# Memory attention and gated convolution on one core: convolution and x by halves of the tokens, for both head groups side by side

## The chip, the cores and the metric

The kernel runs on one core of a Trainium2 chip. The metric is device time in microseconds (us), the median of three runs. A profiled execution of the same program gives the rows below; its own time is named beside its span.

## What is computed

Eight batches, each with 8 heads, 576 tokens, head width 64 and 32 memory slots; then a gated convolution over 512 channels.

```
a    = softmax(phi, over the tokens)                  # [b,h,s,m]
k_m, v_m = a^T k, a^T v                               # [b,h,m,d]
attn = softmax(q k_m^T / 8, over the slots)           # [b,h,s,m]
x    = attn v_m, heads side by side                   # [b,s,512]
gate = sigmoid(sum_k conv_w[k] * x[s-4+k])            # 5 taps per channel
out  = (gate * (x w_val)) w_out                       # [b,s,512]
```

## The kernel before

All tensors are 32 bits wide. The 8 heads form two groups g of 4 heads (4 x 32 slots = 128 partitions); the 576 tokens form two halves s of 288; the 512 channels form four tiles t of 128, two per group. A line of text, `ORDER`, lists every step of all batches, and the steps are issued in that order, so each engine's queue is the list filtered to that engine. A star at a step's end picks its other engine (`pick`, L211).

Per batch b: `slots` (L398) sums a^T[k v 1] per group in 20 matmuls; `slots_scale` (L416) divides by the sum and writes k and v twice each; `slots_turn` (L429) transposes them, two transposes per group; `scores` (L444) makes q k_m^T for one group in 8 matmuls; the softmax steps (`scores_turn` to `soft_turn`, L455 to L509) run on VectorE, ScalarE and GpSimd and end in pT, the attention turned so that slots lie on partitions. `val_rows` (L527) makes v_m w_val, so that `value` (L626) yields x w_val from attn directly, in 6 matmuls per (half, tile). `gated` (L637) multiplies by the gate on VectorE, `gated_high` and `gated_low` split the product into two parts, `project` (L656) multiplies by w_out in 12 matmuls, `place` copies out of PSUM and `store` writes to memory.

The convolution of a pair (b, g) has two forms. `conv` (L569) folds the 5 taps into v (`taps`, L559) and lets TensorE do them: 40 matmuls of 32x64x288 into two `cv` tiles in PSUM, then one sigmoid per tile. `mix` (L591) computes x itself in 8 matmuls of 32x64x292, and the taps are applied from PSUM: `tap` 0 on ScalarE (L607), taps 1 to 4 on VectorE (L611), each 128x576, then `open_gate`. The table `MIXED` (L35) takes `mix` for 8 of the 16 pairs. In `conv` the two halves of one head go to different 64-column sides of the array (`(j - s) % HG`, L576); in `mix` they go to the same side (`divmod(j, 2)`, L596). `conv` therefore leaves half the channels of the second half of the tokens swapped; to match, `val_again` (L551) keeps a copy of 64 channels behind each value tile, and `wo_pair` (L337) builds a second copy of w_out with rows swapped, by 12 transfers from SBUF to SBUF on SyncE's queue. There are two `cv` tiles of two PSUM banks each, and both are used by `conv`, `mix`, `scores` and, at the start, `warm` (matmuls with no use but to keep TensorE busy). Four `b` tiles of one bank serve all the rest. Loads and stores are all issued by SyncE (SP). k and v lie in one buffer per group (`kvs`, L178), so a group's next load waits for `slots` of the batch before.

Of the kernel before, what the change touches and what calls it, by code (L numbers as in the profile page):

```python
# [45 lines left out]
narrow_done.v.0 load_q.0.0 phi_sub.0.1* narrow_round.v.3 scores.0.0 scores_turn.0.0 soft_max.0.0 warm.8 soft_sub.0.0*
warm.2 phi_exp.0.1 narrow_size.v.3 load_kv.0.1 slots.0.1 warm.2 soft_exp.0.0 narrow_bits.v.3 narrow_add.v.1
narrow_done.v.1 warm.2 load_w.o.1 narrow_size.o.1 soft_sum.0.0 soft_inv.0.0 place_taps.1 phi_sub.1 spread_taps.0
narrow_add.v.3 phi_exp.1 slots_inv.0.1 slots_scale.0.1 warm.2 slots_turn.0.1 slots_place.0.1 narrow_done.v.3
narrow_bits.o.1 place_taps.0 soft_mul.0.0* load_q.0.1 load_w.o.3 narrow_size.o.3 warm.2 narrow_round.o.3 taps.0.0  # L50
soft_turn.0.0 load_kv.1.0 narrow_round.o.1 narrow_bits.o.3 scores.0.1 scores_turn.0.1 soft_max.0.1 soft_sub.0.1*
soft_high.0.0 val_rows.0 val_high.0.1 val_high.0.0 narrow_add.o.3 val_low.0.1 load_kv.1.1 val_low.0.0 soft_exp.0.1
soft_sum.0.1 soft_inv.0.1* warm.2 conv.0.0 sigmoid.0.1 turn_taps.0 lay_taps.0 sigmoid.0.0 soft_mul.0.1* narrow_add.o.1
soft_turn.0.1 slots.1.0 slots_inv.1.0 slots_scale.1.0* narrow_done.o.1 slots.1.1 soft_low.0.0* load_phi.2 load_w.o.2
soft_high.0.1* taps.0.1 wo_high.1 conv.0.1 val_again.0.0.vwH val_again.0.1.vwH* load_q.1 slots_inv.1.1
# [5 lines left out]
val_rows.1 scores_turn.1.0 wo_high.2 wo_low.2 wo_pair.1.0 val_high.1.0 scores_turn.1.1 value.0.1.1 gated.0.1.1
gated_high.0.1.0 value.0.1.3 val_again.1.0.vwH* wo_pair.0.1 project.0.0.0 soft_max.1 val_high.1.1 soft_sub.1
gated.0.1.3 val_low.1.1 soft_exp.1 phi_sub.2 project.0.0.3 project.0.0.1 val_low.1.0 place.0.0.1 place.0.0.0*
phi_max.3 soft_sum.1 soft_inv.1 project.0.0.2 place.0.0.3 value.0.1.2 soft_mul.1* phi_exp.2 gated.0.1.2
gated_high.0.1.1 soft_turn.1 load_kv.2.0 keep_v.1.1 gated_low.0.1.0 val_again.1.0.vwL slots.2.1 slots_inv.2.1
place.0.0.2 slots.2.0 phi_turn.3 slots_scale.2.1* wo_pair.0.0 val_again.1.1.vwH* mix.1.1 slots_inv.2.0 tap.1.2.0
gated_low.0.1.1 slots_turn.2.1 phi_top.3 phi_spread.3 keep_v.2.1 slots_scale.2.0 soft_high.1* phi_lay.3 tap.1.2.1
tap.1.2.2 slots_place.2.1 tap.1.3.0 tap.1.2.3 slots_turn.2.0 slots_place.2.0 tap.1.2.4 open_gate.1.2 tap.1.3.1
tap.1.3.2 soft_low.1 wo_pair.1.1 project.0.1.1 place.0.1.1 load_q.2 project.0.1.0 load_kv.3.0 place.0.1.0 store.0.1.0
tap.1.3.3 tap.1.3.4 open_gate.1.3 value.1.1.3 project.0.1.2 value.1.1.2 gated.1.1.3 taps.2.0 gated.1.1.2 place.0.1.2*  # L70
gated_high.1.1.1 value.1.0.2 gated.1.0.2 phi_sub.3 conv.1.0 val_again.1.1.vwL value.1.1.1 sigmoid.1.1 gated.1.1.1
sigmoid.1.0 value.1.1.0 gated.1.1.0 load_phi.4 phi_max.4 scores.2.1 phi_exp.3 scores.2.0 scores_turn.2.1 value.1.0.3
scores_turn.2.0 gated.1.0.3 gated_high.1.1.0 gated_low.1.1.0* value.1.0.1 soft_max.2 project.0.1.3 load_kv.3.1
place.0.1.3 value.1.0.0 store.0.1.1 gated_low.1.1.1 gated.1.0.1 gated.1.0.0 gated_high.1.0.0 store.0.0.0 soft_sub.2
slots.3.0 gated_high.1.0.1 gated_low.1.0.0 gated_low.1.0.1 slots_inv.3.0 slots.3.1 phi_turn.4 slots_scale.3.0
soft_exp.2 slots_inv.3.1 phi_top.4 slots_scale.3.1 soft_sum.2 soft_inv.2 load_kv.4.0 soft_mul.2* val_rows.2
project.1.1.3 place.1.1.3 val_high.2.1 project.1.0.3 val_high.2.0 place.1.0.3 keep_v.3.1 store.0.0.1 soft_turn.2
project.1.0.1 val_again.2.0.vwH load_q.3 val_low.2.0 val_again.2.1.vwH* val_low.2.1 load_phi.5 project.1.1.2
place.1.1.2* place.1.0.1* mix.2.1 slots_turn.3.1 tap.2.3.0 slots_place.3.1 tap.2.3.1 store.1.1.1 tap.2.2.0
slots_turn.3.0 slots_place.3.0 val_again.2.1.vwL* load_kv.4.1 val_again.2.0.vwL phi_spread.4 phi_lay.4 soft_high.2  # L80
project.1.1.1 place.1.1.1 tap.2.2.1 phi_sub.4 phi_exp.4 project.1.0.0 project.1.1.0 place.1.1.0 tap.2.3.2 tap.2.3.3
project.1.0.2 tap.2.3.4 open_gate.2.3 val_rows.3 place.1.0.2 val_high.3.1 store.1.0.1 tap.2.2.2 tap.2.2.3 tap.2.2.4
open_gate.2.2 phi_max.5 soft_low.2 place.1.0.0 val_high.3.0 val_again.3.1.vwH conv.2.0 val_low.3.1 taps.3.0*
val_again.3.0.vwH value.2.0.0 sigmoid.2.0 val_low.3.0 gated.2.0.0 sigmoid.2.1 value.2.0.1 gated.2.0.1 scores.3.0
scores.3.1 scores_turn.3.0 scores_turn.3.1 soft_max.3 val_again.3.1.vwL* gated_high.2.0.0 slots.4.1 slots_inv.4.1
slots_scale.4.1* slots.4.0 slots_inv.4.0 value.2.0.2 slots_scale.4.0* gated.2.0.2 value.2.1.2 gated.2.1.2 value.2.0.3
load_phi.6 store.1.0.0 gated.2.0.3 gated_high.2.0.1* gated_low.2.0.0 gated_low.2.0.1* value.2.1.1 gated.2.1.1
soft_sub.3 soft_exp.3 soft_sum.3 soft_inv.3 value.2.1.3 project.2.0.1 place.2.0.1 soft_mul.3* gated.2.1.3 soft_turn.3
value.2.1.0 project.2.0.0 place.2.0.0 project.2.0.3 gated.2.1.0 gated_high.2.1.0 phi_turn.5 mix.3.1 phi_top.5
place.2.0.3* tap.3.2.0 gated_low.2.1.0* tap.3.3.0 gated_high.2.1.1* gated_low.2.1.1 phi_spread.5 tap.3.2.1 tap.3.2.2  # L90
tap.3.2.3 tap.3.3.1 load_kv.5.1 tap.3.3.2 tap.3.3.3 store.1.1.0 phi_lay.5 slots_turn.4.1 keep_v.4.1 load_kv.5.0
slots_turn.4.0 project.2.0.2 tap.3.2.4 project.2.1.3 place.2.0.2 val_again.3.0.vwL* soft_high.3 phi_sub.5
slots_place.4.0 project.2.1.2 place.2.1.2 load_q.4 project.2.1.0 tap.3.3.4 scores.4.0 slots_place.4.1 scores.4.1
phi_exp.5 scores_turn.4.0 scores_turn.4.1 soft_max.4 val_rows.4 store.2.0.0 place.2.1.3 store.2.1.1 val_high.4.1*
place.2.1.0 project.2.1.1 val_high.4.0 taps.4.0* place.2.1.1 open_gate.3.2 soft_low.3 value.3.0.2 val_again.4.0.vwH
# [626 lines left out]
```

## Time and profile before

| | |
|---|---|
| time, median of 3 runs | 268.93 us (268.8 to 272.24) |
| time of the profiled execution | 271.08 us |
| its span, first to last instruction | 269.3 us |
| TensorE (PE) busy | 250.1 us, 93% |
| VectorE (DVE) busy | 206.9 us, 77% |
| ScalarE (ACT) busy | 140.5 us, 52% |
| GpSimd (POOL) busy | 116.2 us, 43% |
[...]

Busy time counts any moment with at least one instruction in flight; matmuls overlap, so TensorE's price of a step is read from the chain of waits, where steps follow each other without overlap. A 32-bit matmul shows as two records: 8 matmuls of `mix` are "x16". "Start to start" is the distance of the starts of successive instructions.

### The profile page before, as it was taken

Reading aid. Unit: us, or ns where it says so; the run is one execution under the profiler, and the core shown is the slowest. Engines: PE = TensorE matmul, PEld = TensorE weight load, DVE = VectorE, ACT = ScalarE, POOL = GpSimd, SP = SyncE. Lnnn points to the kernel's source line nnn. Section 1 sums busy time; section 2 is a strip of 40 time slices with the busy share of each in tenths; the row PEclk is TensorE's granted clock in tenths of the full one; section 3 lists DMA queues with packets and bytes.
Section 4 is the critical chain, followed back from the end, with each engine's and each line's share of the span. In section 5 each row is a group of like instructions: output and inputs, shape, how many; then the busy total and the mean of one; then the engine's idle time right before and its main releaser. Section 6 shows DMA issues by size and latency. Waiting matters only on the chain.

```text
span 269.3 us, 7274 instructions
## 1 busy us (share of the span) xinstructions
PE 250.1 (93%) x3096; PEld 216.0 (80%) x3096; DVE 206.9 (77%) x338; ACT 140.5 (52%) x245; POOL 116.2 (43%) x94
## 2 busy tenths in 40 slices
PE   0599959995999999999999999999999999999995
PEld 0387757793988887798789996999879878899994
DVE  2678978996759979789886777789577987898831
ACT  3726764762745558445685346636458565364210
POOL 4466613892921616323635540743237144461200
PEclk9999989998999999999999999999999999999999
DMA  6999987698681992099407268088143210102123
GB/s 203 407 357 355 320 339 247 156 240 234 249 318 60 333 352 99 15 325 347 167 12 217 103 223 267 0 287 334 44 142 127 77 56 2 44 2 88 46 88 131
DMA packets 13232, 49.91 MB, mean 185 GB/s; under 512 B 1673, under 2 KB 2185, under 8 KB 10257
## 3 DMA queue, kind: packets, MB, share of 16 engines
q1 hardware_dynamic: 13200, 49.46, 53.7%
q8 instruction: 24, 0.39, 0.6%
q14 instruction: 8, 0.06, 0.1%
HBM read 37.92 MB, written 9.44 MB: 176 GB/s over the span
## 4 chain that ended last, share of the span: by engine, by line
PE 83%; DMA 10%; issue 2%; ACT 2%; SPq 1%; DVE 1%; DVEq 0%; ACTq 0%
PE b L661 36%; PE b L632 18%; PE cv L577 8%; DMA kv<-in_kv_dram 8%; PE b L403 7%; PE cv L597 4%; PE cv L449 3%; PE b L532 2%; DMA e<-in_phi_dram 2%; PE b L433 2%; PE cv L226 1%; PE b L360 1%; SPq L259 1%; ACT hH L216 1%; DVE h L640 0%
## 5 line engine op out<-in xcount | busy, mean ns | idle before, releaser
L661 PE MATMUL b<-hL,woH 128*128 128x288 f32 x256 | 76.6, 299 | 0.0
L661 PE MATMUL b<-hH,woL 128*128 128x288 f32 x256 | 75.5, 295 | 0.0
L661 PE MATMUL b<-hH,woH 128*128 128x288 f32 x256 | 75.4, 294 | 0.0
L219 POOL TENSOR_TENSOR hL<-h,hH 128x576 fp32r<-128x576 f32 x22 | 32.6, 1488 | 60.0 <-ACT hH L216 32.2
L611 DVE SCALAR_TENSOR_TENSOR gate<-cv,cwP,gate 128x576 f32<-128x576 f32 x64 | 50.0, 813 | 5.9 <-ACT gate L607 4.8
L661 PEld LDWEIGHTS b<-hL,woH 128*128 128x128 f32 x256 | 48.0, 187 | 2.8 <-issue 1.0
L661 PEld LDWEIGHTS b<-hH,woH 128*128 128x128 f32 x256 | 48.2, 188 | 0.0
L661 PEld LDWEIGHTS b<-hH,woL 128*128 128x128 f32 x256 | 48.1, 188 | 0.0
L216 ACT COPY o<-b 128x288 f32<-128x288 f32 x48 | 18.7, 399 | 49.4 <-PE b L661 32.8
L640 DVE TENSOR_TENSOR h<-b,gate 128x288 f32<-128x288 f32 x64 | 27.9, 452 | 19.1 <-PE b L632 15.8
L632 PE MATMUL b<-pL,vwH 128*128 128x288 f32 x128 | 29.0, 308 | 0.0
L632 PE MATMUL b<-pH,vwH 128*128 128x288 f32 x128 | 27.3, 294 | 0.0
L632 PE MATMUL b<-pH,vwL 128*128 128x288 f32 x128 | 27.3, 294 | 0.0
L403 PE MATMUL b<-kv,e 128*32 128x129 f32 x640 | 21.8, 287 | 5.8 <-DMA kv<-in_kv_dram 3.1
L403 PEld LDWEIGHTS b<-kv,e 128*32 128x32 f32 x640 | 18.6, 139 | 8.9 <-issue 4.8
L632 PEld LDWEIGHTS b<-pL,vwH 128*128 128x128 f32 x128 | 20.1, 188 | 6.2 <-issue 2.4
L219 POOL TENSOR_TENSOR pL<-pT,pH 128x1152 fp32r<-128x1152 f32 x7 | 18.7, 2673 | 14.1 <-DVE pH L216 9.8
L577 PE MATMUL cv<-pT,taps 32*64 32x288 f32 x640 | 22.0, 410 | 0.1
L479 POOL TENSOR_TENSOR st<-st,mm 128x1152 f32<-128x1152 f32 x7 | 14.9, 2134 | 15.9 <-DVE mm L472 15.0
L216 ACT CAST hH<-h 128x576 fp32r<-128x576 f32 x21 | 13.9, 673 | 14.0 <-DVE h L640 14.0
L389 POOL TENSOR_TENSOR e<-e,mxa 128x1280 f32<-128x1280 f32 x7 | 17.2, 2464 | 8.7 <-ACT mxa L216 8.7
L632 PEld LDWEIGHTS b<-pH,vwL 128*128 128x128 f32 x128 | 20.5, 188 | 0.0
(87 smaller groups left out, 414.1 us busy)
## 6 DMA issues: line engine op xcount, KB each, us to landing
kv<-in_kv_dram SPq DMA_DIRECT2D x16, 1032.0 KB, 7.6
out_dram<-o SPq DMA_DIRECT2D x30, 288.0 KB, 2.4
q<-in_q_dram SPq DMA_DIRECT2D x7, 1152.0 KB, 8.4
e<-in_phi_dram SPq DMA_DIRECT2D x7, 640.0 KB, 6.4
kv<-in_kv_dram SPq DMA_DIRECT2D x16, 129.0 KB, 8.3
raw<-in_w_out_dram SPq DMA_DIRECT2D x4, 512.0 KB, 8.0
...
```

Of the source, the lines that this page charges most:

```text
L216: eng.copy(out=out, in_=x) if eng is nc.scalar else eng.tensor_copy(out=out, in_=x)
L219: eng.tensor_tensor(out=out, in0=x, in1=hi.bitcast(F32), op=ALU.subtract)
L389: eng.tensor_tensor(out=t, in0=t, in1=mxa.unsqueeze(3).to_broadcast(list(t.shape)), op=ALU.subtract)
L403: nc.tensor.matmul(km[j * M:(j + 1) * M, 0:2 * D + 1], lhsT=e[:, g, j * M:(j + 1) * M, c], rhs=x[:, c, j, :], start=(c == 0), stop=(c == C ...
L449: nc.tensor.matmul(sc[j * M:(j + 1) * M, s, 0:HALF], lhsT=live["kvT", b, g][rows, 0, j * M:(j + 1) * M], rhs=live["q", b][rows, g, j, :], ...
L479: eng.tensor_tensor(out=st, in0=st, in1=spread(live["mm", b, g], st), op=ALU.subtract)
L577: nc.tensor.matmul(cv[t][x * D:(x + 1) * D, s, 0:HALF], lhsT=w[rows, i, :], rhs=p[rows, g, s * HALF + i:(s + 1) * HALF + i], start=(i == 0 ...
L597: nc.tensor.matmul(cv[t][x * D:(x + 1) * D, s, 0:PAD + HALF], lhsT=live["taps", b, g][rows, 0, :], rhs=pTs[b % 2][rows, g, s * HALF:(s + 1 ...
L611: nc.vector.scalar_tensor_tensor(out=gt, in0=x, scalar=w, in1=gt, op0=ALU.mult, op1=ALU.add)
L632: nc.tensor.matmul(vp[:, 0:HALF], lhsT=a[:, t // PG, n:n + P], rhs=p[:, g, s * HALF:(s + 1) * HALF], start=(i == 0), stop=(i == len(parts) ...
L640: nc.vector.tensor_tensor(out=h[:, i], in0=live["vp", b, s, t][:, 0:HALF], in1=live["gate", b, t][:, s], op=ALU.mult)
L661: nc.tensor.matmul(ps[:, 0:HALF], lhsT=w[:, t, n * P:(n + 1) * P], rhs=a[:, t % 2], start=(i == 0), stop=(i == len(parts) - 1))
```

## The change

`conv` and `mix` now run per (batch, half of the tokens) with both head groups side by side, and which head goes to which side of the array depends on (head + group). No channels are swapped between halves any more: the host lays the last four heads out in the order 5, 4, 7, 6 in w_val, conv_w and w_out. `val_again`, `keep_v`, `wo_pair` and the second copies of w_out are gone. `mix` is taken for 12 of the 16 (batch, half) pairs (was 8 of 16 (batch, group) pairs): both halves in batches 3 to 7, one half in batches 1 and 2. One `gate` tile now holds the two channel tiles of a group for one half, and as every channel tile has its own tap weights, each tap is two instructions of 128x288 (was one of 128x576).

v is written once per batch for both groups (`kvd[:, G, g]`), so `slots_turn` makes three transposes per batch, and `slots_scale` two instructions per group. k and v loads leave out the last 64 tokens, which come in one transfer per batch for both groups (`load_rest`, 264 KB); the main loads rotate over three buffers. `kvd` has 3 buffers (2), `st` 2 (1). In batch 0 the softmax runs by halves too, so it needs q of both groups at its start. `ORDER` is new throughout; by its stars, VectorE has 5 `place` copies (16), 6 `gated_high` (11), 4 `gated_low` (10), 5 `soft_sub` (2), 4 `soft_mul` (7), 1 `soft_high` (4), 0 `val_high` (2), 3 `slots_scale` (9); the rest of each kind is ScalarE's or GpSimd's. `warm` has 12 matmuls (32).

```diff
-MIXED = {(1, 1), (2, 1), (3, 1), (4, 1), (5, 1), (6, 1), (7, 0), (7, 1)}
+KVS = 3
...
-mix.5.1 tap.5.2.0 tap.5.2.1 store.4.0.0 tap.5.3.0 tap.5.3.1 project.4.0.3 tap.5.3.2 tap.5.3.3 tap.5.3.4 place.4.0.3
+place.4.0.1 project.4.0.3 place.4.0.3 tap.5.1.1.4 project.4.0.2 soft_high.5 tap.5.1.0.3 tap.5.1.0.4 mix.5.0
...
     def load_kv(b, g):
-        t = kvs[g]
-        nc.sync.dma_start(out=t[:, 0:C - 1], in_=kv[b, g, 0:S - KL].rearrange("(p c) n -> p c n", c=C - 1))
-        nc.sync.dma_start(out=t[0:KL, C - 1], in_=kv[b, g, S - KL:])
+        t = kvs[(b * G + g) % KVS]
+        nc.sync.dma_start(out=t, in_=kv[b, g])
+    def load_rest(b):
+        nc.sync.dma_start(out=rests[b % 2], in_=rest[b])
...
-    def wo_pair(i, g):
-        nc.sync.dma_start(out=b[0:D], in_=a[D:P])
-        for t in range(PG):
-            nc.sync.dma_start(out=b[D:P, t], in_=a[0:D, (t + 1) % PG])
...
-    def slots_turn(b, g):
-        for x in range(2):
-            nc.tensor.transpose(out=ps[:, x], in_=live["kvd", b, g][:, x], identity=ident)
+    def slots_turn(b):
+        for x in range(G + 1):
+            nc.tensor.transpose(out=ps[:, x], in_=kvd[:, x].rearrange("p y d -> p (y d)"), identity=ident)
...
-    def val_again(b, g, n):
-        high(pick(nc.gpsimd, nc.scalar), live[n, b, g][:, gs, HG * D:], x[:, gs, 0:D])
...
-    def mix(b, g):
-        for s in range(2):
+    def mix(b, s):
+        for g in range(G):
             for j in range(HG):
-                t, x = divmod(j, 2)
-                nc.tensor.matmul(cv[t][x * D:(x + 1) * D, s, 0:PAD + HALF], lhsT=live["taps", b, g][rows, 0, :],
+                rows, x = slice(j * M, (j + 1) * M), (j + g) % 2
+                nc.tensor.matmul(cv[g][x * D:(x + 1) * D, j // 2, 0:PAD + HALF], lhsT=live["kvd", b][rows, G, g],
                                  rhs=pTs[b % 2][rows, g, s * HALF:(s + 1) * HALF + PAD], start=True, stop=True)
...
-    def tap(b, t, i):
-        x, w = live["cv", b, t][:, :, i:i + HALF], cwP[:, i, t:t + 1]
-            nc.vector.scalar_tensor_tensor(out=gt, in0=x, scalar=w, in1=gt, op0=ALU.mult, op1=ALU.add)
+    def tap(b, s, g, i):
+        for t in range(PG):
+            x, w = live["cv", b, s, g][:, t, i:i + HALF], cwP[:, i, g * PG + t:g * PG + t + 1]
+            if i == 0:
+                nc.scalar.activation(out=gt[:, t], in_=x, func=AF.Identity, scale=w)
+            else:
+                nc.vector.scalar_tensor_tensor(out=gt[:, t], in0=x, scalar=w, in1=gt[:, t], op0=ALU.mult, op1=ALU.add)
...
-            n = t % PG * P + (s * D if swapped(b, t // PG) else 0)
+            n = t % PG * P
```

How the instructions stand, at three places. First TensorE in batch 5 before, from the transposes of batch 6 to the first matmuls of a `project` behind `mix.5.1`; `conv.5.0` follows 67 rows later, behind five projections and two values.

```order
L433 MATMUL b<-ident,kvd 128x128 x2
L360 MATMUL b<-ident,mx 128x128 x2
L597 MATMUL cv<-pT_76,taps 64x292 x8
L661 MATMUL b<-hL,woH_88 128x288
L661 MATMUL b<-hH,woL_90 128x288
```

After, from `mix.5.1` to the next projection (L350 and L393 are `phi_turn` and `slots` of later batches); `mix.5.0` (L591 again) follows after 36 rows of L653, that is three projections.

```order
L591 MATMUL cv<-pT_76,kvd 64x292 x8
L350 MATMUL b<-ident,mx 128x128 x2
L393 MATMUL b<-kv_78,e 32x129 x16
L393 MATMUL b<-rest_81,e 32x129 x4
L393 MATMUL b<-kv_79,e 32x129 x16
L393 MATMUL b<-rest_81,e 32x129 x4
L624 MATMUL b<-pL,vwH 128x288 x2
L624 MATMUL b<-pH,vwL 128x288 x2
L624 MATMUL b<-pH,vwH 128x288 x2
L653 MATMUL b<-hL,woH 128x288
```

In place of a `conv` (L577, x40) a second `mix` follows the first, three projections, one value and one batch's `slots` behind it, and it needs the same two `cv` tiles.

Second VectorE at the same place, before: L611 are the taps of `mix.5.1`, L640 the multiplications by the gate.

```order
L219 TENSOR_TENSOR hL<-h,hH 128x576
L611 SCALAR_TENSOR_TENSOR gate<-cv,cwP,gate 128x576 x6
L216 COPY o<-b 128x288
L611 SCALAR_TENSOR_TENSOR gate<-cv,cwP,gate 128x576 x2
L640 TENSOR_TENSOR h<-b,gate 128x288 x2
L216 CAST hH<-h 128x576
L216 COPY o<-b 128x288
```

After: L604 are the taps, L632 the multiplications by the gate; the x6 and the x10 are the 16 instructions of `mix.5.1`, the x8 the first 8 of `mix.5.0`.

```order
L632 TENSOR_TENSOR h<-b,gate 128x288 x3
L357 TENSOR_REDUCE top<-b 128x2
L604 SCALAR_TENSOR_TENSOR gate<-cv,cwP,gate 128x288 x6
L400 TENSOR_SCALAR ri<-b 128x1
L402 RECIPROCAL ri<-ri 128x1
L632 TENSOR_TENSOR h<-b,gate 128x288
L604 SCALAR_TENSOR_TENSOR gate<-cv,cwP,gate 128x288 x10
L400 TENSOR_SCALAR ri<-b 128x1
L402 RECIPROCAL ri<-ri 128x1
L604 SCALAR_TENSOR_TENSOR gate<-cv,cwP,gate 128x288 x8
```

The 8 instructions of 576 columns have become 16 of 288, and a second 16 follow close behind, with fewer copies and casts between them.

Third SyncE's queue, before: k and v of batch 2 (`load_kv.2.1`, L241 and L242 on kv_80, and `load_kv.2.0` on kv_78), with `wo_pair` (L339, L341) around the second.

```order
L236 DMA e<-in_phi_dram 128x1280
L241 DMA kv_80<-in_kv_dram 128x2064
L242 DMA kv_80<-in_kv_dram 64x516
L339 DMA woL_91<-woL_90 64x1024
L341 DMA woL_91<-woL_90 64x512 x2
L339 DMA woH_89<-woH_88 64x1024
L341 DMA woH_89<-woH_88 64x512 x2
L241 DMA kv_78<-in_kv_dram 128x2064
L242 DMA kv_78<-in_kv_dram 64x516
```

After: L235 on kv_79 and kv_80 are k and v of batch 2, L240 the rest of batch 2, L255 the last w_out load.

```order
L235 DMA kv_78<-in_kv_dram 128x2064
L255 DMA raw<-in_w_out_dram 128x1024
L235 DMA kv_79<-in_kv_dram 128x2064
L245 DMA q<-in_q_dram 128x2304
L235 DMA kv_80<-in_kv_dram 128x2064
L230 DMA e<-in_phi_dram 128x1280
L240 DMA rest_81<-in_rest_dram 128x516
```

No transfer from SBUF to SBUF stands ahead of the loads of batch 2, and the first of them goes to a buffer that batch 0 has left.

## Rows read from the trace of the kernel before

**Rows 1.** Page, parts 1 and 2: span; busy us (share) and instructions; granted clock by 40 slices.
```profile
span 269.3 us, 7274 instructions
PE 250.1 (93%) x3096; PEld 216.0 (80%) x3096; DVE 206.9 (77%) x338; ACT 140.5 (52%) x245; POOL 116.2 (43%) x94
PEclk9999989998999999999999999999999999999999
```

**Rows 2.** Chain of waits, start us, us, engine, tile, line: one of each TensorE step.
```profile
76.30 2.61 PE cv L577 x80
...
78.91 1.79 PE b L632 x12
...
80.70 1.13 PE cv L449 x32
...
85.99 2.36 PE b L403 x80
...
96.34 1.15 PE cv L597 x16
...
147.33 6.40 PE b L661 x48
153.73 0.22 PE b L433 x2
```

**Rows 3.** Busy by stretch: us, then PE, PEld, DVE, ACT, POOL busy (instructions), PEclk, DMA share, GB/s.
```profile
0.00:65.87 65.87, 49.78 (x706) 40.21 (x708) 50.02 (x82) 36.81 (x66) 36.02 (x39) 0.97 0.89 284
65.87:242.26 176.39, 176.39 (x2213) 152.56 (x2214) 142.47 (x230) 97.23 (x166) 77.29 (x53) 0.99 0.46 164
242.26:269.30 27.04, 23.90 (x184) 23.18 (x184) 14.38 (x26) 6.48 (x14) 2.86 (x2) 1.00 0.23 88
```

**Rows 4.** SyncE's waits: who waited for whom, us, times, longest.
```profile
SPq L339 <- ACT vwH L216: 7.5, 1, 7.5
```

**Rows 5.** Chain of waits, the two stalls of TensorE.
```profile
35.44 2.72 issue
38.16 2.52 PE b L403 x41
...
52.41 0.60 SPq L341
...
53.05 10.82 DMA kv<-in_kv_dram
...
63.92 1.34 PE b L403 x40
...
65.87 2.15 PE cv L597 x16
```

**Rows 6.** Busy by stretch, as rows 3: behind the second stall, and VectorE's densest 20 us.
```profile
65.00:70.00 5.00, 5.00 (x44) 3.14 (x35) 2.93 (x7) 1.81 (x4) 2.52 (x1) 0.66 0.95 355
120.00:140.00 20.00, 20.00 (x257) 16.72 (x259) 18.12 (x26) 11.81 (x20) 9.37 (x7) 1.00 0.56 198
```

**Rows 7.** Timeline of VectorE, start us, us, line, output<-inputs, count [idle before].
```profile
68.84 6.66 DVE L611 SCALAR_TENSOR_TENSOR gate<-cv,cwP,gate 128x576 f32<-128x576 f32 x8 [1.44 <-ACT gate L607]
...
145.77 0.81 DVE L640 TENSOR_TENSOR h<-b,gate 128x288 f32<-128x288 f32 x2
...
236.30 5.88 DVE L611 SCALAR_TENSOR_TENSOR gate<-cv,cwP,gate 128x576 f32<-128x576 f32 x8
```

**Rows 8.** Groups by form on VectorE and ScalarE: count, busy us, mean ns, idle before.
```profile
L611 DVE SCALAR_TENSOR_TENSOR gate<-cv,cwP,gate 128x576 f32<-128x576 f32 x64 | 50.0, 813 | 5.9 <-ACT gate L607 4.8
L640 DVE TENSOR_TENSOR h<-b,gate 128x288 f32<-128x288 f32 x64 | 27.9, 452 | 19.1 <-PE b L632 15.8 <-ACT gate L616 1.6 <-issue 1.0
L506 DVE TENSOR_TENSOR st<-st,ss 128x1152 f32<-128x1152 f32 x5 | 6.8, 1358 | 0.2
L219 DVE TENSOR_TENSOR hL<-h,hH 128x576 fp32r<-128x576 f32 x10 | 7.6, 767 | 0.1
L506 DVE TENSOR_TENSOR st<-st,ss 128x576 f32<-128x576 f32 x2 | 1.5, 756 | 0.0
L216 DVE COPY o<-b 128x288 f32<-128x288 f32 x16 | 7.0, 451 | 9.5 <-PE b L661 9.5
L216 DVE CAST hH<-h 128x576 fp32r<-128x576 f32 x11 | 5.0, 458 | 0.3
L607 ACT ACTIVATE gate<-cv,cwP 128x576 f32<-128x576 f32 x16 | 11.2, 741 | 10.6 <-PE cv L597 10.5
L216 ACT COPY o<-b 128x288 f32<-128x288 f32 x48 | 18.7, 399 | 49.4 <-PE b L661 32.8 <-issue 15.7 <-ACT mxa L216 0.8
```

More of the change, by code (lines that the diff above doesn't have):

```diff
@@ L46 @@
[L46 to L55, printed above, removed]
@@ L61 @@
[L61 to L70, printed above, removed]
@@ L71 @@
[L71 to L95, printed above, removed]
@@ new lines @@
+slots_place.3 phi_lay.4 project.1.1.0 tap.2.1.0.1 tap.2.1.0.2 tap.2.1.0.3 gated_high.1.0.1 gated_low.1.0.1 place.1.1.0
+store.1.1.0 tap.2.1.0.4 project.1.1.3 tap.2.1.1.0 tap.2.1.1.1 soft_high.2 place.1.1.3 phi_sub.4 soft_low.2
+project.1.0.0 place.1.0.0 tap.2.1.1.2 tap.2.1.1.3 phi_exp.4 val_rows.3 val_high.3.0 val_high.3.1 scores.3.1
+scores_turn.3.1 tap.2.1.1.4 open_gate.2.1.1 load_kv.4.1 store.1.1.1 val_low.3.0 project.1.0.2 scores.3.0 place.1.0.2
+scores_turn.3.0 open_gate.2.1.0 soft_max.3 slots.4.0 slots.4.1 phi_turn.5 soft_sub.3* taps.2.1 soft_exp.3 conv.2.0
@@ new lines @@
+tap.3.1.0.4 value.2.1.2 gated.2.1.0 gated.2.1.3 gated.2.1.2 phi_exp.5 gated_high.2.1.0 gated_low.2.1.0
+gated_high.2.0.1 load_kv.5.1 tap.3.1.1.1 scores.4.1 tap.3.1.1.2 scores_turn.4.1 val_rows.4 place.1.0.1 gated_low.2.0.1
+slots.5.1 gated_high.2.1.1 slots_inv.5.1 val_high.4.0 val_low.4.0 slots_scale.5.1* slots.5.0 tap.3.1.1.3 store.0.1.1
+slots_inv.5.0 slots_scale.5.0* load_rest.6 scores.4.0 scores_turn.4.0 soft_high.3 gated_low.2.1.1 project.2.1.1
+slots_turn.5 tap.3.1.1.4 slots_place.5 place.2.1.1 phi_turn.6 mix.3.0 tap.3.0.0.0 soft_max.4 soft_sub.4 phi_top.6
@@ new lines @@
+open_gate.5.1.0 val_high.6.0 value.5.1.3 gated.5.1.3 value.5.0.0 phi_sub.7 phi_exp.7 val_low.6.0 tap.5.0.1.3
+tap.5.0.1.4 store.4.0.0 project.4.1.2 place.4.1.2 load_q.7 value.5.1.1 soft_sub.6 gated_high.5.1.1 gated.5.0.0
+gated_low.5.1.1 slots.7.1 soft_exp.6 slots_inv.7.1 slots_scale.7.1* soft_sum.6 slots.7.0 slots_inv.7.0
+slots_scale.7.0* project.4.1.3 project.4.1.1 soft_inv.6 soft_mul.6* place.4.1.3 value.5.1.0 soft_turn.6 place.4.1.1
+value.5.0.3 store.4.1.0 mix.6.1 slots_turn.7 gated.5.1.1 gated.5.1.0 gated_high.5.1.0* open_gate.5.0.1 tap.6.1.0.0
```

367 lines of the change are left out of this document (200 added, 167 removed).

## The prediction

> **What bounds the kernel now.** The page first: TensorE is busy 93% of a 269.3 us span, VectorE 77%, and the granted clock is near full all through [rows 1]. Cut at the first `mix` (65.87 us) and the last (242.26 us), the middle of 176.4 us has TensorE in flight for 176.39 us and VectorE for 142.5, that is 81% [rows 3]. The chain of waits says the same: there it is TensorE, step behind step. So in the middle the end is set by the sum of TensorE's steps, and their prices are read from that chain [rows 2]: `conv` 2.61 us (x80), `mix` 1.15 (x16), a `value` 0.80 (1.59 for x12 records), a `project` 1.60 (6.40 for x48), both groups' `scores` 1.13, both groups' `slots` 2.36, a pair of transposes 0.22. Ahead of the middle TensorE stands still twice: 2.72 us at 35.44, then on the load of k and v of batch 2, issued at 53.05 and landed at 63.87, 2.8 us [rows 5]. That load was late because SyncE waited 7.5 us, for ScalarE, with a transfer of `wo_pair` ahead of it [rows 4].
>
> **The change, part by part.** All sums are against the profiled execution's span of 269.3 us.
>
> *TensorE, number of convs.* Eight `conv` and eight `mix` cost 8 x 2.61 + 8 x 1.15 = 30.1 us. Four `conv` and twelve `mix` at today's price would cost 24.2.
>
> *TensorE, price of a mix.* Here the code matters more than the count. A matmul of 32 rows x 64 columns takes one of 4 x 2 places of the array. `conv` uses all 8: its 40 matmuls are 5 rounds of 8, 2.61 us, 0.52 per round. `mix` before sends head j to side j % 2 in both halves, so its 8 matmuls share 4 places and make two rounds: 1.15 us. After, the side is (j + g) % 2, and the 8 matmuls lie on 8 different places: one round. No row shows such a `mix`. Its bounds are 0.52 (a round of `conv`) and 1.15 (no gain); `scores` of one group is 8 matmuls of 288 on 8 places (64 rows x 32 columns), and two of them take 1.13 us [rows 2], so I take 0.57. Twelve at 0.57 and four `conv` make 17.3 us: 12.8 less than before. The bounds of the price leave 13.4 to 5.9.
>
> *TensorE, transposes.* Three per batch in place of four: 8 x 0.11 = 0.9 us less.
>
> *SyncE and the second stall.* `wo_pair` is gone from the queue, and the first load of batch 2 goes to a third buffer. It no longer waits for anything made after batch 0. [...] What is late next in this place is nothing of SyncE's that I see.
>
> *The start.* Batch 0 by halves needs q of both groups before its first softmax, and the loads up to k and v of batch 1 are 11,320 KB against 10,680 KB, counted over the queue. The 10,680 KB had landed at 38.16 us [rows 5], about 0.28 MB per us, so 640 KB are 2.3 us; 0 if other work hides them. I take 1.5 us more. The 20 `warm` matmuls dropped lie in waits for loads; they cost nothing either way.
>
> Without any wait for VectorE the span would be 269.3 - 12.8 - 0.9 - 4.5 + 1.5 = 252.6 us.
>
> *VectorE, the taps.* 64 instructions of 128x576 become 192 of 128x288. A tap that follows a tap of the same `gate` tile starts 0.83 us after it ((6.66 - 0.82) / 7), one that follows a tap of another tile 0.72 us ((5.88 - 0.82) / 7) [rows 7]. Between them lies the wait for the write before. After, the two channel tiles of a tap alternate, so the second distance holds. A product of 1152 columns takes 1.358 us, one of 576 0.756: 0.30 per 288 columns [rows 8]. So half the columns give 0.72 - 0.30 = 0.42. Bounds: 0.36, the distance of two gate multiplications of 288 columns ((0.81 - 0.45) [rows 7]), and 0.54, the 0.83 less 0.30. At 0.42 all taps take 81 us instead of 51.
>
> *VectorE, what is taken off.* 11 copies at 0.451, 5 casts at 0.458 and 6 subtractions at 0.767 go to ScalarE and GpSimd, two products at 1.36 to GpSimd [rows 8]; with the smaller ones, less three `soft_sub` more, some 20 us. ScalarE gains about 19 (11 copies at 0.399, 48 first taps at some 0.40 for 16 at 0.741 [rows 8], casts), to 160 us, 63% of the span: no bound. GpSimd stays near 119.
>
> *VectorE against TensorE.* In the middle, 7 mixes before and 11 after: 56 taps at 0.79 leave (44 us), 176 at 0.423 come (74 us), 15.6 of the 20 us go: 142.5 + 30.2 - 15.6 = 157.1 us. TensorE's own middle is 176.4 - 1.7 (clock) - 12.2 (12.8 less the mix behind the cut) - 0.8 = 161.7 us. VectorE would have to be busy 97%. In its densest 20 us today it is busy 18.12, 91%, without holding anybody up [rows 6]. The order shows where it binds: between `mix.5.1` and `mix.5.0` TensorE has 0.57 + 0.22 + 2.36 + 0.80 + 3 x 1.60 = 8.7 us of work, and VectorE 16 x 0.42 + 4 x 0.36 + some 0.7 = 8.9 us before the `cv` tiles are free. Behind a late `mix` stand the projections, and behind a late tap the gate multiplications that free the `b` tiles. If VectorE must idle 5.5% of the time (between the 3% that fit and the 9%), the middle is 157.1 / 0.945 = 166.2 us: 4.6 us of waits. The bounds are 0 and 157.1 / 0.906 - 161.7 = 11.7.
>
> Sum: 252.6 + 4.6 = 257.2 us of span. The profiled execution took 271.08 us, 1.8 over its span and 2.15 over the median of 268.93, so the median comes to 257.2 + 1.8 - 2.15 = 256.9, say 257.
>
> [...]
>
> **The rivals.**
> *Dearer taps.* If a tap takes 0.45, as one gate multiplication measured from its start to its end [rows 8], the middle of VectorE is 161.9 us and at 94.5% 171.3: 5 us more, 262. For it: taps carry waits for ScalarE. Against it: the 0.72.
> *The mixes don't get faster.* If row groups that write the same PSUM bank shut each other out, `mix` stays at 1.15: TensorE 7.0 more, the waits nearly gone, 260. Against it: in `conv` heads 0 and 1 write one bank from two row groups, and a round still takes 0.52 [rows 2].
> [...]
> *Waits in long pieces.* If the waits come as four of 2.7 us, each is followed by a slow clock of 1.7 us as behind the second stall [rows 5, 6]: 4 x 4.4 in place of 4.6 gives 270. For it: VectorE's work comes in runs of 16 taps. Against it: at 5 us in all most waits are short.
> *Slower: VectorE bound.* If the alternating taps don't overlap and each takes 0.54, VectorE's middle is 177.7 us, at 94.5% 188: 26 us of waits, 279 in all. It is slower by over 2% from 0.517 us per tap on. Against it: one run of 8 in the trace overlaps.
>
> **How the numbers follow.** The forecast (250 to 262 by the bounds above: no waits and a start that costs nothing, or 10 us of waits) 0.58; dearer taps 0.12; mixes at 1.15 0.08; waits in long pieces 0.12; VectorE bound 0.10. Two per cent, about what a measurement here can tell from no change, is 263.6 and 274.3. Below 263.6 lie the forecast, most of the cheap mixes' rival (0.07) and some of the dearer taps (0.08): 0.73. Within: 0.05 + 0.12 = 0.17, rounded with the rest of the mixes. Above: 0.10. The range from 250 to 268 leaves out the last rival, half of the long waits and a little below: 0.18.
>
> **What would show it.** A `mix` of 0.5 to 0.6 us in the chain of waits; taps 0.42 apart; no wait of TensorE on k and v between 55 and 66 us; VectorE above 90% busy between the first and the last `mix`, and short waits of `mix`, `scores` and `value` on VectorE's taps and gate products. The forecast is wrong if TensorE waits for something else for many us (ScalarE's first taps, `slots_place`, GpSimd's `soft_mul`), or if the start takes over 3 us more.

## The result and the profile after

| | before | after |
|---|---|---|
| time, median | 270.59 us (268.8 to 273.93) | 257.65 us (256.84 to 258.4) |
| ratio, with its interval | | 0.9542 [0.9445, 0.964] |
| time of the profiled execution | 271.08 us | 258.32 us |
| its span | 269.3 us | 256.5 us |
| TensorE busy | 250.1 us, 93% | 234.4 us, 91% |
| VectorE busy | 206.9 us, 77% | 218.2 us, 85% |
| ScalarE busy | 140.5 us, 52% | 159.9 us, 62% |
| GpSimd busy | 116.2 us, 43% | 118.3 us, 46% |

The change makes the kernel faster by 4.6%. Predicted were 257 us; measured were 257.65. (The time of before moves a little with the chip and the day; times below are read through their ratio to the runs of before beside them.)

The page of the kernel after, parts 1 and 2 (answers to [rows 1]): span, busy time and share, granted clock in 40 slices.

```profile
span 256.5 us, 6783 instructions
PE 234.4 (91%) x2792; PEld 201.7 (79%) x2792; DVE 218.2 (85%) x431; ACT 159.9 (62%) x294; POOL 118.3 (46%) x82
PEclk9999999999999999999999999999999999999999
```

The chain of waits of after (start us, us, engine, tile, line), one of each convolution step and of `scores`, answers to [rows 2]:

```profile
60.83 0.68 PE cv L591 x16
...
74.32 1.13 PE cv L443 x32
...
101.21 2.61 PE cv L578 x80
...
119.18 0.65 PE cv L443 x16
```

A `mix` (L591) takes 0.68 us in place of 1.15, a `conv` (L578) 2.61 as before (the other one in the middle takes 3.15, see below). The two rows of `scores` (L443) show how my price of a `mix` went wrong: both groups' scores together take 1.13, which I halved to 0.57, but one group's alone takes 0.65. A second round right behind the first adds only the other 0.48. The trace of before had such a row, too:

```profile
218.21 0.65 PE cv L449 x16
```

Busy by stretch in after, cut at the first and the last `mix` as [rows 3] (us, then PE, PEld, DVE, ACT, POOL busy with instructions, granted clock, DMA share, GB/s):

```profile
0.00:60.83 60.83, 44.32 (x668) 34.99 (x671) 47.07 (x79) 35.68 (x62) 32.47 (x34) 1.00 0.81 311
60.83:229.27 168.44, 166.08 (x1950) 143.48 (x1953) 156.84 (x321) 116.87 (x217) 82.78 (x47) 1.00 0.43 159
229.27:256.50 27.23, 23.97 (x191) 23.29 (x190) 14.29 (x32) 7.35 (x17) 3.08 (x3) 1.00 0.21 77
```

Beside [rows 3] the start is 5.0 us shorter (60.8 for 65.9), the middle 8.0 (168.4 for 176.4), and the tail unchanged. In the middle VectorE's share goes from 81 to 93%, and TensorE, which never stood still there, now does for 2.4 us.

### The profile page after: what moved, and what is told of

Its sections match the earlier page's. It is cut to its first block, busy times and chain, and to the rows that moved or that the text cites. A ratio compares the mean times of both kernels' runs of the same rounds, so it can differ in the third digit from the quotient of the medians.

```text
span 256.5 us, 6783 instructions
## 1 busy us (share of the span) xinstructions
PE 234.4 (91%) x2792; PEld 201.7 (79%) x2792; DVE 218.2 (85%) x431; ACT 159.9 (62%) x294; POOL 118.3 (46%) x82
## 4 chain that ended last, share of the span: by engine, by line
PE 65%; DVE 19%; DMA 7%; ACT 4%; issue 2%; SPq 1%; POOL 0%; DVEq 0%; ACTq 0%
PE b L653 29%; PE b L624 16%; PE b L393 5%; PE cv L591 3%; PE cv L578 3%; DMA kv<-in_kv_dram 3%; PE cv L443 3%; DVE st L488 2%; DMA raw<-in_w_out_dram 2%; DVE mm L481 2%; PE b L543 2%; DVE st L515 2%; DMA out_dram<-o 2%; DVE pT L521 2%; DVE ss L499 2%
## 5 line engine op out<-in xcount | busy, mean ns | idle before, releaser
L604 DVE SCALAR_TENSOR_TENSOR gate<-cv,cwP,gate 128x288 f32<-128x288 f32 x192 | 84.6, 506 | 4.3 <-ACT gate L602 4.1
L653 PE MATMUL b<-hL,woH 128*128 128x288 f32 x256 | 77.4, 302 | 1.7 <-DVE h L632 1.7
L653 PE MATMUL b<-hH,woL 128*128 128x288 f32 x256 | 75.5, 295 | 0.0
L653 PE MATMUL b<-hH,woH 128*128 128x288 f32 x256 | 75.1, 293 | 0.0
L213 POOL TENSOR_TENSOR hL<-h,hH 128x576 fp32r<-128x576 f32 x28 | 40.3, 1450 | 52.6 <-ACT hH L210 38.6
L653 PEld LDWEIGHTS b<-hL,woH 128*128 128x128 f32 x256 | 48.1, 188 | 7.8 <-issue 3.8
L653 PEld LDWEIGHTS b<-hH,woL 128*128 128x128 f32 x256 | 48.1, 188 | 0.0
L653 PEld LDWEIGHTS b<-hH,woH 128*128 128x128 f32 x256 | 48.1, 188 | 0.0
L210 ACT COPY o<-b 128x288 f32<-128x288 f32 x59 | 22.8, 400 | 32.1 <-PE b L653 25.1
L632 DVE TENSOR_TENSOR h<-b,gate 128x288 f32<-128x288 f32 x64 | 27.4, 444 | 8.2 <-PE b L624 4.1
L602 ACT ACTIVATE gate<-cv,cwP 128x288 f32<-128x288 f32 x48 | 21.2, 504 | 6.9 <-PE cv L591 6.8
L213 POOL TENSOR_TENSOR pL<-pT,pH 128x1152 fp32r<-128x1152 f32 (+1 forms) x8 | 20.3, 2544 | 8.9 <-ACT pH L210 6.7
L210 ACT CAST hH<-h 128x576 fp32r<-128x576 f32 x26 | 17.4, 674 | 6.7 <-DVE h L632 6.7
L609 ACT ACTIVATE gate<-gate 128x576 f32<-128x576 f32 x24 | 16.3, 687 | 7.6 <-DVE gate L604 7.6
L288 POOL TENSOR_TENSOR hH<-hH,hL 128x512 int32<-128x512 int32 (+1 forms) x9 | 12.1, 1353 | 18.5 <-DVE hH L274 11.8
L624 PEld LDWEIGHTS b<-pH,vwH 128*128 128x128 f32 x128 | 20.5, 188 | 0.0
L393 PE MATMUL b<-kv,e 128*32 128x129 f32 x512 | 17.5, 277 | 2.1 <-DMA kv<-in_kv_dram 2.1
```

What stands on the lines that cost most here:

```text
L210: eng.copy(out=out, in_=x) if eng is nc.scalar else eng.tensor_copy(out=out, in_=x)
L213: eng.tensor_tensor(out=out, in0=x, in1=hi.bitcast(F32), op=ALU.subtract)
L288: nc.gpsimd.tensor_tensor(out=a, in0=a, in1=r, op=ALU.add)
L393: nc.tensor.matmul(km[j * M:(j + 1) * M, 0:2 * D + 1], lhsT=e[:, g, j * M:(j + 1) * M, c], rhs=x[:, c, j, :] if c < C - 1 else rests[b % 2 ...
L602: nc.scalar.activation(out=gt[:, t], in_=x, func=AF.Identity, scale=w)
L604: nc.vector.scalar_tensor_tensor(out=gt[:, t], in0=x, scalar=w, in1=gt[:, t], op0=ALU.mult, op1=ALU.add)
```

## Where the time went: the experiments

Three questions were put to the chip: what the cheaper `mix` is worth, whether VectorE now sets the pace of the middle, and why the start came 3.7 us earlier than I had reckoned (first `mix` forecast at 65.87 - 2.8 + 1.5 = 64.6 us, measured at 60.8). "Before" and "after" are the two kernels, and each ratio is to runs of before on the same chip.

### The places of a mix, in the kernel before and in the kernel after

`b1_mix_places`: the kernel before, with the second half of a head on the other side of the array (half of the channels then come out swapped).

```diff
-                t, x = divmod(j, 2)
+                t, x = j // 2, (j + s) % 2
```

> The kernel before with one edit: in mix the side of the array is (head + half) % 2 in place of head % 2, so the 8 matmuls of a mix lie on 8 places in place of 4. The second half of the tokens of the mixed pairs then carries its heads swapped, so the values differ; the work is the same. My theory: a mix falls from 1.15 to 0.68 us (as in the changed kernel), and since TensorE is never waited out in the middle, all 8 x 0.47 = 3.8 us come off the time: ratio 0.986 to the kernel before. Rival (row groups that write one PSUM bank shut each other out): mix stays at 1.15 and the time the same.

Measured: 265.95 us, 0.9863 [0.9812, 0.9915].

`a1_mix_four`: the kernel after, with `mix` on four places again.

```diff
-                rows, x = slice(j * M, (j + 1) * M), (j + g) % 2
+                rows, x = slice(j * M, (j + 1) * M), j % 2
```

> The changed kernel with one edit: the side of the array in mix is head % 2 for both groups, so a mix takes 4 places in two rounds, as before. Heads of the second group come out swapped in the mixed halves; the work is the same. My theory: a mix goes from 0.68 to 1.15 us, 12 x 0.47 = 5.6 us on TensorE, of which what TensorE waits for VectorE today (some 5 us in the middle) hides a part: 3 to 5.6 us more, 260.5 to 263. Rival, VectorE sets the pace of the middle: at most 1 us more, 257 to 258.5.

Measured: 261.8 us, 0.9702 [0.9649, 0.9755], some 4.3 us more than after by the ratios.

The chain of waits of `b1_mix_places`, and then of `a1_mix_four`:

```profile
93.74 0.68 PE cv L597 x16
```

```profile
109.94 1.14 PE cv L591 x16
```

Eight places take 0.68 and four take 1.14 to 1.15, in either kernel. So the kernel before could have had 8 x 0.47 = 3.8 us, nearly a third of the change's 12.4 us (0.0458 x 270), by an edit of one expression; measured were 3.7 (2.3 to 5.1 by the interval). In `a1_mix_four` 12 x 0.46 = 5.5 us of TensorE's work come back, and 4.3 of them reach the end (4.9 beside the second measurement of after, below). Its middle alone, with 11 of the 12, grows by less:

```profile
61.18:231.48 170.30, 169.60 (x1947) 145.96 (x1948) 157.61 (x322) 116.95 (x217) 82.80 (x47) 1.00 0.43 157
```

170.3 us against 168.4 and 167.3 are 1.9 to 3.0 of 5.1 us; the others fall into waits that were there before. So TensorE's own steps bind the middle for between two fifths and nine tenths, and VectorE alone does not pace it: that rival allowed 1 us at most.

### The load of batch 2

`b2_kv_early`: the kernel before, with the load of k and v ahead of `wo_pair` in the queue.

```diff
-load_kv.2.1 phi_lay.2 ... soft_turn.1 load_kv.2.0 keep_v.1.1
+load_kv.2.1 load_kv.2.0 phi_lay.2 ... soft_turn.1 keep_v.1.1
```

> The kernel before with one step moved: load_kv.2.0 stands directly behind load_kv.2.1 on SyncE's queue, ahead of the transfers of wo_pair. My theory: TensorE's wait for k and v of batch 2 (2.8 us) and the slow clock behind it (1.7 us) go, 4.5 us less: ratio 0.983. Rival: the wait moves to the next late thing (the exponential of batch 2, or the transfers of wo_pair ahead of project), and 0 to 2 us come off.

Measured: 267.0 us, 0.9886 [0.984, 0.9932]: 3.1 us by the ratio, in the profiled execution 5.3. The chain no longer holds the load, and in this execution the first `mix` starts 4.1 us earlier than in [rows 5]:

```profile
60.00 0.37 DVE h L640
60.37 1.29 DVE pT L511
...
61.80 1.21 PE cv L597 x16
```

Just ahead of that `mix` VectorE ends the turn of the softmax (L511, pT): as soon as the load is on time, the softmax of batch 1 is next in line. That limits what an earlier load alone can give. How much it gives differs between executions: in `b3_both`, next, whose start is the same, the profiled one has its first `mix` at 64.92, with a granted clock of 0.80 from 40 to 50 us where `b2_kv_early` had all of it.

`b3_both`: both edits in the kernel before (channels as in `b1_mix_places`).

> The kernel before with two edits that the runs of each alone have priced: the mixes on eight places (0.9863 of before) and the load of k and v of batch 2 ahead of wo_pair (0.9886). Theory (the two gains lie in different stretches and add): 0.975, 263 to 264 us beside 270, so that a little over half of the change's 4.6 per cent is had without new halves, and the other 2.1 per cent are the four conv fewer, 4 x (2.61 - 0.68) = 7.7 us of TensorE, less 2 to 3 us that VectorE and loads take back. Rival (the early load's gain is taken by the next wait once the mixes are faster): 0.986, 266 us.

Measured: 263.87 us, 0.9789 [0.9729, 0.9849]. The two ratios multiply to 0.9751, which lies inside this interval, and the 0.986 of the rival doesn't: the gains add, or nearly. So a little under half of the change's gain (2.1 of 4.6%) has nothing to do with halves.

### Is VectorE the bound in the middle?

Three kernels around the one after: less VectorE work, more of it, and work moved back to TensorE. The added and the dropped tap:

```diff
     def tap(b, s, g, i):                                     # a3_tap_less
+        if i == KT - 1:
+            return
...
-        for t in range(PG):                                  # a4_tap_more
+        for t in [*range(PG)] * (2 if i == KT - 1 else 1):
```

`a3_tap_less`:

> The changed kernel without the last of the five taps in the mixed halves, so its gates lack that tap of the convolution: 48 of 192 tap instructions of VectorE are gone, 44 of them between the first and the last mix, about 18.7 us of VectorE's 156.8 us there at 0.424 us from start to start. Theory (of the 168.4 us between the first and the last mix TensorE's own work is about 163 and the other 5.5 us are waits for VectorE): the waits shrink to about 1 us, 4 to 5 us less in all, a median of 253 to 254 us. Rival (TensorE alone sets the time, its waits come from loads, stores and ScalarE): nothing, 257 to 258 us. Second rival (VectorE sets the pace): up to 15 us less.

Measured: 255.94 us, 0.9486 [0.9417, 0.9555].

`a4_tap_more`:

> The changed kernel with the last tap of the mixed halves done twice, so its gates hold that tap double: 48 tap instructions more, 44 of them between the first and the last mix, 18.7 us more of VectorE there, 175.5 us in all. Theory (VectorE is within a few us of being the bound): the stretch becomes 175.5 us at a busy share of 93 to 97 per cent, 181 to 189 us, 12 to 20 us more than now: 270 to 278 us, slower than the kernel before the change or level with it. Rival (TensorE sets the time and VectorE has slack): below 5 us more, up to 262 us.

Measured: 271.03 us, 1.0025 [0.9991, 1.0058].

`a5_mix8` takes `conv` for the first half of batches 3 to 6; in `ORDER`:

```diff
-mix.3.0 tap.3.0.0.0 ... tap.3.0.1.4 ... open_gate.3.0.0 ... open_gate.3.0.1
+conv.3.0 sigmoid.3.0.0 ... sigmoid.3.0.1
```

> The changed kernel with conv in place of mix for the first half of batches 3 to 6, so 8 of 16 halves are mixed as before the change. TensorE's own work grows by 4 x (2.61 - 0.68) = 7.7 us, VectorE's falls by some 64 taps at 0.424 us, 27 us, all of it between the first and the last mix. Theory (about 5.5 us of waits for VectorE there): the waits go and pay most of it, 2 to 4 us more than the changed kernel, 260 to 262 us. Rival (no waits for VectorE to be had back): the full 7.7 us, 265 us. Second rival (VectorE sets the pace): faster than the changed kernel.

Measured: 263.95 us, 0.9771 [0.9717, 0.9825].

The middle in each, cut as above: `a3_tap_less`, `a4_tap_more`, `a5_mix8`, and the second profile of after (`after_again`, below).

```profile
61.27:226.80 165.53, 164.03 (x1951) 142.52 (x1953) 140.77 (x278) 116.52 (x217) 82.84 (x47) 1.00 0.44 162
```

```profile
62.30:240.01 177.71, 169.75 (x1944) 143.73 (x1943) 172.59 (x362) 116.14 (x215) 82.75 (x47) 1.00 0.41 151
```

```profile
62.45:235.04 172.59, 172.29 (x2207) 150.09 (x2209) 131.77 (x256) 111.76 (x202) 90.56 (x55) 1.00 0.42 155
```

```profile
60.72:228.00 167.28, 166.16 (x1959) 143.63 (x1958) 156.94 (x322) 116.88 (x217) 82.99 (x47) 1.00 0.43 160
```

Read the first number and the fifth: 140.8 us of VectorE give a middle of 165.5, 156.9 give 167.3 to 168.4, 172.6 give 177.7. On the left 16 us less VectorE bring 2 to 3 us; on the right 16 us more cost 9 to 10. The kernel stands at the bend between two bounds, still on TensorE's side. By the ratios, against both measurements of after, the dropped tap was worth 0.9 to 1.5 us, which their intervals do not tell from nothing, where I had expected 4 to 5; the doubled one cost 13 to 13.6, as expected. And on the right VectorE is busy 172.59 of 177.71 us, 97%: it can be packed closer than the 94.5% of my sum.

`a5_mix8` says the same from the other side. It adds 4 x (2.61 - 0.68) = 7.7 us to TensorE and takes 25 us from VectorE, and 6.2 to 6.8 us of the 7.7 arrive at the end. Its middle is only 4.2 to 5.3 us longer; its start is 1.6 longer, with nothing changed in it. So the waits for VectorE that could be given back were 0.9 to 1.5 us by the times of both kernels, 2 to 3.5 by their middles: some 1 to 3 us. One piece can be seen: the first `conv` of the middle takes 3.15 us in both profiles of after, and 2.61 once the tap is dropped (the rows are of after and of `a3_tap_less`):

```profile
69.38 3.15 PE cv L578 x80
```

```profile
69.82 2.61 PE cv L578 x80
```

The theory of `a5_mix8` (waits of 5.5 us that would pay most of it) fell; its rival, the full price, was nearer.

What fills the middle beside these 1 to 3 us? TensorE's own steps there come to about 163 us, as an estimate: the middle of `b1_mix_places` is 171.90 us with TensorE in flight all through, less four `conv` (10.4), with four and a half more `mix` (3.1), the six fewer transpose records (0.7), and by the place of the cut twelve projection records less and six value records more (0.9 with a transpose). That leaves 4.3 to 5.4 us above 163, close to the 4.6 in my sum, of which VectorE's taps explain between a fifth and two thirds. The rest is in short pieces. One could be named: in the chain of after, ScalarE waits for a store, since there are three output tiles.

```profile
127.91 0.41 ACT o L210
128.34 4.31 DMA out_dram<-o
132.75 0.41 ACT o L210
133.20 2.74 PE b L624 x18
...
135.94 0.68 PE cv L591 x16
```

`c1_o4_kv` gives a fourth output tile, and issues a load ahead of a store behind which it stood in the first profile of after.

```diff
-... "o": 3 ...
+... "o": 4 ...
-store.1.1.0 tap.2.1.0.4 ... open_gate.2.1.1 load_kv.4.1 store.1.1.1
+load_kv.4.1 store.1.1.0 tap.2.1.0.4 ... open_gate.2.1.1 store.1.1.1
```

> The changed kernel with a fourth buffer for the output tiles and the load of k and v of batch 4 issued ahead of a store. In the chain of waits of the changed kernel that load started at 90.92 us behind a store that waited for ScalarE, and TensorE waited 1.3 us for it; later ScalarE waited for a store to free an output tile. Theory: the 1.3 us wait goes and a part of the later one, 1 to 3 us less, 255 to 257 us. Rival (the waits are taken over by VectorE's taps of the same stretch, which are as late): no difference, 257 to 258 us.

Measured: 256.39 us, 0.9505 [0.9439, 0.9571], which can't be told from after (0.9542 and 0.952). In its trace the store is gone from the chain, and the way from that `mix` to the one before is 13.1 us (121.39 to 134.53) where both profiles of after have 13.7. That is the half microsecond that the fourth tile is worth. The 1.3 us that TensorE waited for the load of batch 4 isn't there in the second profile of after either, so it is chance and not a cost of the order. What remains of the 4.3 to 5.4 us, 1 to 3, stays open; no run took it apart.

### Why the start is shorter

Between 10 and 40 us the DMA engines are busy all the time in every kernel (a share of 0.98 to 1.02), and loads land at 357 GB/s in before and at 405 in after. The kernel before loads the last 64 rows of k and v of each group in a transfer of 129 KB to 64 partitions, the one after those of both groups in one of 258 KB to 128 partitions (the 264 KB named above, in units of 1024). The theory: the start goes by that rate, and the rate by that shape. Two halves should then bring the first `mix` 2 to 3 us later than 60.83, and the time to 259 to 260.5 us; with another cause, such as the order of the loads, nothing should move.

`a2_rest_halves`, and once more as `a2_again`: after, with the 258 KB as two transfers to 64 partitions.

```diff
-        nc.sync.dma_start(out=rests[b % 2], in_=rest[b])
+        for x in range(2):
+            nc.sync.dma_start(out=rests[b % 2][x * D:(x + 1) * D], in_=rest[b, x * D:(x + 1) * D])
```

> The changed kernel with one edit: the last 64 tokens of k and v of a batch come in two transfers of 64 partitions (129 KB each), as before, in place of one of 128. The start of the changed kernel was 3.7 us earlier than I forecast. [...]

Measured: 258.68 us, 0.9573 [0.952, 0.9626]. Its profiled execution, with 372 GB/s and the first `mix` at 65.70 us, was the longest of its four (261.96 us, the others 257.8 to 259.4), so nothing was settled. It was run again beside the unaltered kernel, `after_again`:

> The changed kernel once more, unaltered, beside the two runs with other loads. Every theory expects 257 to 258 us, the first mix at 61 to 62 us, and 395 to 407 GB/s between 10 and 40 us, where the DMA engines are busy all the time.

Measured: 256.81 us, 0.952 [0.9454, 0.9585].

> The changed kernel with each load of the last rows of k and v as two transfers to 64 partitions of 129 KB, as in the kernel before, in place of one of 258 KB to 128 partitions; a second look. Its first profile moved 372 GB/s between 10 and 40 us and had its first mix at 65.7 us; the kernels of before moved 357 to 364, the others of the changed family 395 to 407. Theory (transfers to 64 partitions are slow, and their shape is what makes the start shorter): 365 to 380 GB/s again, first mix 2 to 4 us later than in the unaltered kernel. Rival (the first profile was disturbed): 395 to 407 GB/s, first mix within 1 us.

Measured: 259.55 us (259.44 to 260.0), 0.9623 [0.9574, 0.9672], against 256.01 to 257.57 of `after_again` beside it: 2.7 us more, where the first measurement gave 0.8 by the ratios. And with the cause made large, `a7_kv_halves`, where each load of k and v goes as two transfers to 64 partitions:

```diff
-        nc.sync.dma_start(out=t, in_=kv[b, g])
+        for x in range(2):
+            nc.sync.dma_start(out=t[x * D:(x + 1) * D], in_=kv[b, g, x * D:(x + 1) * D])
```

> The changed kernel with each load of k and v of 1032 KB as two transfers of 516 KB to 64 partitions each. Theory (a transfer to 64 partitions is slow): four such loads lie between 10 and 40 us, 4.1 of 12.1 MB; at some 260 GB/s, the dips seen beside the small halves, in place of 405 they take 6 us more: first mix at 65 to 68 us, below 350 GB/s between 10 and 40 us, 3 to 6 us slower in all. Rival (two halves in flight together cover all partitions and go at full rate): no change, within 1 us.

Measured: 270.57 to 279.56 us in ten executions; the three shortest give 1.0087 [1.003, 1.0143], and by them it is about 15 us more than after.

The stretch from 10 to 40 us in before, `after_again`, `a2_again` and `a7_kv_halves` (the last two columns are DMA share and GB/s):

```profile
10.00:40.00 30.00, 26.20 (x380) 21.03 (x384) 25.30 (x43) 17.84 (x32) 16.56 (x13) 0.96 1.01 357
```

```profile
10.00:40.00 30.00, 23.12 (x418) 17.17 (x424) 25.04 (x48) 19.20 (x36) 16.29 (x12) 0.94 1.00 405
```

```profile
10.00:40.00 30.00, 22.62 (x345) 17.46 (x345) 22.20 (x39) 16.41 (x31) 15.25 (x12) 0.89 0.98 355
```

```profile
10.00:40.00 30.00, 20.96 (x222) 14.55 (x221) 17.79 (x31) 11.26 (x23) 11.78 (x9) 0.72 1.02 276
```

The engines are full each time, and what they bring falls with the bytes that go to 64 partitions: 405, 355, 276 GB/s. That it is the shape, and not that the transfers are smaller, can be seen inside `a7_kv_halves`. From 10 to 22 us the halves of 516 KB are in flight. From 24 to 27.5 those of batch 0 have landed (the load issued behind them did at 24.07), the next are issued only at 27.41, and loads of 512 and 576 KB to 128 partitions remain:

```profile
10.00:22.00 12.00, 7.44 (x71) 6.50 (x70) 6.33 (x9) 4.32 (x9) 7.26 (x5) 1.00 1.01 243
```

```profile
24.00:27.50 3.50, 3.38 (x51) 2.85 (x52) 0.75 (x5) 1.73 (x3) 0.00 (x0) 0.50 1.02 411
```

That is 243 against 411 GB/s. The first `mix` of `after_again`, `a2_again` and `a7_kv_halves`:

```profile
60.72 0.68 PE cv L591 x16
```

```profile
63.70 0.68 PE cv L592 x16
```

```profile
72.71 0.68 PE cv L592 x16
```

It comes later with the lower rate, but not because of the rate as a whole. The chain of waits of `after_again`, then of `a2_again`, shows where the 3.0 us between them arise:

```profile
8.74 10.71 DMA rest<-in_rest_dram
...
19.50 1.60 PE b L393 x48
...
23.10 1.25 PE cv L443 x32
```

```profile
9.46 11.66 DMA rest<-in_rest_dram
...
21.25 2.81 PE b L394 x48
...
26.10 1.22 PE cv L444 x32
```

From 8.7 us on one load stands in these chains: the last 64 rows of k and v of batch 0. As two halves it is issued 0.7 us later and lands 1.7 us later. TensorE has then stood still for 1.85 us, its granted clock is 0.56 from 21 to 24 us, and `slots` (L393, L394) takes 2.81 us in place of 1.60. At batch 0's `scores` (L443, L444) the 3.0 us are complete. From there to the first `mix` neither chain holds a load, only VectorE's and ScalarE's steps and TensorE's own, and both take 37.6 us, at 405 GB/s and at 355. `a1_mix_four`, `a3_tap_less` and `c1_o4_kv` take 37.6 as well (`a4_tap_more` and `a5_mix8`, at a lower clock, 38.3 and 38.4). So behind 23 us the start of the kernel after goes by its compute steps and not by the rate at which loads land. In `a7_kv_halves`, and in the longest execution of `a2_rest_halves`, a later load stands in the chain, too: there the loads are late enough.

So the shape of one small load is worth 3.0 us in this pair of profiles. Beside the other kernels with the whole load, whose first `mix` comes at up to 62.45 us, it is 1.3, and by the times 0.8 to 2.7. That it explains the 3.7 us by which the start beat my forecast is not shown: `b2_kv_early` loads the same halves as before and has its first `mix` at 61.80, 1.0 us behind that of after. A rival that no run tested is the order of the queue. The kernel before issues the k and v of batch 0's second group at 13.36 us, behind a load that waits for its buffer, and this load stands in its chain; the one after issues both groups' by 8.7 us.

```profile
13.36 10.33 DMA kv<-in_kv_dram
```

The rival in `a7_kv_halves`, that two halves in flight together make up for it, fell with `a7_kv_halves`. What makes a transfer to 64 partitions slow no run shows, only that it is: 243 GB/s with halves in flight against 411 without, and 276 against 405 over the 30 us.

## Why the prediction was right, step by step

The forecast itself came true, a TensorE-bound kernel at 257 us, and none of the rivals. But three of its terms were off and cancelled. That it came within 0.7 us is therefore luck.

- **Convs and mixes, -12.8 us.** Four `conv` at 2.61 and twelve `mix` at 0.68 make 18.6, so -11.5. The step that failed is the price of 0.57, half of a pair; it should have been that of a single round (0.65 to 0.68). 1.3 us too much gain.
- **Transposes, -0.9.** Not tested by itself; the six fewer records in the middle are 0.7 us by their price.
- **Second stall, -4.5.** This is the wait of 2.8 us and 1.7 us (5 x 0.34) for the clock behind it, 0.66 in the 5 us from 65 [rows 6], in which the first `mix` took 2.15 us [rows 5]. No run shows the 4.5 itself. The load is gone from the chain before the first `mix`, and the granted clock stays full in that stretch. The same done alone in the kernel before gave 3.1 us in the timed runs, 5.3 in the profiled one. The mechanism holds, the size lies within these. ([rows 5] show the load's 10.82 us and not the 2.8 that TensorE waited for it; that is this row of before:)

```profile
PE b L403 <- DMA kv<-in_kv_dram: 2.8, 1, 2.8
```

- **Start, +1.5.** It was 2.2 us less in place of 1.5 more. I counted bytes up to k and v of batch 1 and let the start grow with them. That path was wrong: the chain of after holds no load behind 8.3 us, that of `after_again` only the last rows of batch 0, and then the softmax steps. (That the 10,680 KB had landed at 38.16 us was my inference; [rows 5] name no load for that wait.) This is the worst term, the only one of the wrong sign. A part of the 3.7 us may belong to the stall, which took 4.1 us and not 2.8 off the first `mix` in the profile of `b2_kv_early`.
- **Taps, 0.42 from start to start.** In VectorE's timeline of after, the answer to [rows 7]:

```profile
137.95 4.33 DVE L604 SCALAR_TENSOR_TENSOR gate<-cv,cwP,gate 128x288 f32<-128x288 f32 x10
```

  (4.33 - 0.51) / 9 = 0.424 us. A single tap lasts 0.506 by its group, so the rival that took the time from start to end for the price was wrong in kind: the next tap starts 0.08 us before the last has ended. All 192 together are busy 84.6 us, 0.44 each, where I had 81.

```profile
L604 DVE SCALAR_TENSOR_TENSOR gate<-cv,cwP,gate 128x288 f32<-128x288 f32 x192 | 84.6, 506 | 4.3 <-ACT gate L602 4.1
```

- **VectorE in the middle, 157.1 us.** Measured 156.84. Two errors hide in it: the taps there take some 3 us more than my 74 (176 at 0.44), so some 3 us more than my 15.6 were taken off.
- **Waits, +4.6.** The middle lies 4.3 to 5.4 us above TensorE's own steps, so the size was right; the reason given, VectorE, is shown for only 1 to 3 us of it (`a3_tap_less`, `a5_mix8`). A share of 94.5% as VectorE's ceiling was too low: `a4_tap_more` ran it at 97%. With 97%, VectorE's 157 us fit into 162, and there would have been next to no waits in the sum. (The 1.59 us for two `value` is not the row shown in [rows 2], which has 1.79; the chain of before has both, and no term of the sum rests on it.)

Against the profiled span: 257.2 forecast, 256.5 and 254.9 measured in two profiles. By stretch, for the first of them: the start came 3.7 us earlier than forecast, the middle took 168.4 for 166.2 (half of that the mixes), and the tail 27.2 for 26.4.

Of the rivals, "the mixes don't get faster" would have needed row groups that shut each other out of a bank; 0.68 against 1.14 for the same matmuls on four places shows that they don't here. "Waits in long pieces" didn't come: the longest wait of TensorE in the middle is 1.3 us, and the clock is full there. "VectorE bound" is real and near: `a4_tap_more` is that case, 10% more VectorE work in the middle and the whole gain is gone.
